# Windowed ALiBi attention feeding a Swish-gated MLP: loading and transposing q and k by head pair, adding bias and mask with a TensorE table in two batches, and gating the loads

## The chip, the cores and the metric

One NeuronCore of one Trainium2 chip runs the whole program. The metric is the device time of one execution in microseconds (us). Lower is better. The profile is one execution recorded by the hardware profiler, and its span is one to two us shorter than the measured time of the same run. All times compared here are of runs in the fast state, except where one slow run is named (a run more than 1.5% above the fastest of its kernel is called slow and left out). The profiled run of the kernel before took 376.3 us (its runs lie around 374).

Engine names in the profile: PE is TensorE matmul, PEld its weight load, DVE is VectorE, ACT is ScalarE, POOL is GpSimd, SPq is the queue of the sync engine that issues most DMAs. The granted clock is the share of its full clock that TensorE was given.

## The reference

```python
# q, k, v: (8 batches, 8 heads, 576 tokens, 64)
scores = q @ k.T / sqrt(64)
rel    = pos[:, None] - pos[None, :]
scores = where((rel >= 0) & (rel < 128), scores - slope[h] * abs(rel), -1e9)   # window 128
attn   = softmax(scores) @ v
x      = attn as (4608 tokens, 512)
h      = x @ w_in                       # 512 x 2048
out    = (h * sigmoid(beta * h)) @ w_out   # 2048 x 512
```

## The kernel before

q, k and v are float32 in memory and are loaded by blocks of 128 tokens for all heads. One row of a head is 64 floats, so one packet is 256 bytes. GpSimd casts to bf16, TensorE transposes, VectorE copies the transposes out of PSUM.

```python
fst_pool = ...tile_pool(name="fst", bufs=16)          # float32 staging for q, k and v
psum_h: 2 banks (MoE tiles)   psum_o: 2 (output tiles)
psum_s: one score tile of 2 banks                      psum_t: 2 (everything else)

def load_rows(src, b, sb):                             # one block of 128 tokens, all heads
    f = fst_pool.tile([P, H, D], F32, ...)
    nc.sync.dma_start(out=f[0:rows], in_=src[b, :, P*sb : P*sb+rows, :].rearrange("h p d -> p h d"))

def SC(b, m, p):                                       # one score tile: head pair p, half m
    sps = psum_s.tile([P, 2, 512], F32, ...)
    ... nc.tensor.matmul(o, lhsT=k, rhs=q, start=True, stop=True)
    for e in range(2):                                 # four exponentials, ALiBi as their bias
        for half, cols in ((0, slice(0, OWN[m])), (1, slice(OWN[m], 512))):
            nc.scalar.activation(out=pt[:, e, cols], in_=sps[:, e, cols], func=Exp,
                                 scale=qscale, bias=bias[:, half, h:h+1])
    nc.vector.tensor_tensor(out=pt[:], in0=pt[:], in1=masks[m][:], op=mult)

def HS(g, j):   # MoE tile: 4 matmuls of 512 columns, tanh on ACT, multiply on DVE
def OS(g, i, n) # output tile: 16 matmuls of 512 columns in 4 steps
```

The tokens go through the MoE in nine groups of 512. `att` is the list of the attention steps: T (transposition), SC (score tile), PV, and X (transposition of the result). The main loop puts these steps between the MoE steps. Group 0 has 16 MoE tiles and no output tiles. It must also hold the attention of batch 1 and the first part of batch 2.

```python
for g in range(NTG):
    ... items = HS tiles of g, and from g = 1 on the OS tiles of g - 1
    start, span_ = done, len(items) - 3
    for n, it in enumerate(items):
        it()
        while done < min(target, start + (target - start) * (n + 1) // span_):
            att[done][1](); done += 1
```

The softmax here doesn't subtract the row's maximum and nothing guards it: scores larger than these inputs give would overflow.

Of the kernel before, what the change touches and what calls it, by code (L numbers as in the profile page):

```python
# [10 lines left out]
ALU = mybir.AluOpType  # L11
ACTF = mybir.ActivationFunctionType
# [6 lines left out]
def kernel(  # L19
# [17 lines left out]
    NP = H // 2  # L37
    NQB = 5
# [10 lines left out]
    REF = 63.5  # L49

    const = ctx.enter_context(tc.tile_pool(name="const", bufs=1))
    ident = const.tile([P, P], BF16, name="ident")
    identf = const.tile([NFF, NFF], F32, name="identf")
    bflat = const.tile([NFF, P], F32, name="bflat")
    beta_h = const.tile([P, NFF], F32, name="beta_h")
    one = const.tile([P, 1], BF16, name="one")
    masks = [const.tile([P, 2, 512], BF16, name=f"mask{m}") for m in range(2)]
# [9 lines left out]
    fst_pool = ctx.enter_context(tc.tile_pool(name="fst", bufs=16))  # L67
    bst_pool = ctx.enter_context(tc.tile_pool(name="bst", bufs=4))
    pt_pool = ctx.enter_context(tc.tile_pool(name="ptp", bufs=11))
    xn_pool = ctx.enter_context(tc.tile_pool(name="xn", bufs=2))  # L70
# [3 lines left out]
    psum_h = ctx.enter_context(tc.tile_pool(name="psum_h", bufs=2, space=bass.MemoryType.PSUM))  # L74
    psum_o = ctx.enter_context(tc.tile_pool(name="psum_o", bufs=2, space=bass.MemoryType.PSUM))
# [4 lines left out]
    def load_rows(src, b, sb):  # L80
        rows = ROWS[sb]
        f = fst_pool.tile([P, H, D], F32, name="fst", tag="fst")
        nc.sync.dma_start(  # L83
            out=f[0:rows],
            in_=src[b, :, P * sb : P * sb + rows, :].rearrange("h p d -> p h d"),
        )
        return f

    staged = {}

    def load_qk(b, sb):
        rows = ROWS[sb]
        fq = load_rows(q, b, sb)
        fk = load_rows(k, b, sb)
        t = bst_pool.tile([P, 2, H, D], BF16, name="bst", tag="bst")
        nc.gpsimd.tensor_copy(out=t[0:rows, 0], in_=fq[0:rows])  # L96
        c = nc.gpsimd.tensor_copy(out=t[0:rows, 1], in_=fk[0:rows])  # L97
        staged[b, sb] = t
        return c

    def load_v(b, sb):
        rows = ROWS[sb]
        f = load_rows(v, b, sb)
        return nc.gpsimd.tensor_copy(out=VS[b % 2][0:rows, sb, :, 0:D], in_=f[0:rows])  # L104

    make_identity(nc, ident[:])
    nc.sync.dma_start(out=bflat[:], in_=moe_beta.rearrange("(j p) -> j p", p=P))
    make_identity(nc, identf[:])
    nc.vector.memset(one[:], 1.0)
# [3 lines left out]
    )  # L113

    low = dict(compare_op=ALU.is_ge, fill=0.0, base=0, channel_multiplier=-1)
    up = dict(compare_op=ALU.is_ge, fill=0.0, base=-1, channel_multiplier=1)

    def fill(m, at, n, w, sign, how):
        for e in range(2):
            nc.gpsimd.affine_select(  # L120
                out=masks[m][:, e, at : at + n * w].rearrange("p (n w) -> p n w", w=w),
                in_=bass.AP(tensor=one.tensor, offset=one[:].offset,
                            ap=[list(one[:].ap[0]), [0, n], [0, w]]),
                pattern=[[0, n], [sign, w]], **how,
            )


    fill(0, 0, 2, P, 1, low)
    fill(0, 256, 2, P, -1, up)

    fill(1, 0, 1, P, 1, low)
    fill(1, 128, 1, 64, 1, low)
    fill(1, 192, 1, P, 1, low)
    fill(1, 320, 1, 64, -1, up)
    fill(1, 384, 1, P, -1, up)
    for h in range(H):
        for half in range(2):
            nc.vector.tensor_scalar(
                out=bias[:, half, h : h + 1], in0=kpos[:], scalar1=-(REF + half * P),
                scalar2=slopes[h], op0=ALU.add, op1=ALU.mult,  # L140
            )
# [4 lines left out]
    for sb in range(3):  # L146
        load_qk(0, sb)
# [10 lines left out]
    bps = psum_t.tile([P, NFF], F32, name="bps", tag="t")  # L158
    nc.tensor.transpose(out=bps[:], in_=bflat[:], identity=identf[:])
    nc.vector.tensor_scalar_mul(beta_h[:], bps[:], 0.5)  # L160
# [4 lines left out]
    def T(b, sb):  # L165
        rows = ROWS[sb]
        src = staged.pop((b, sb))
        tps = psum_t.tile([P, 2, NP, P], BF16, name="tps", tag="t")
        for i in range(2):
            for p in range(NP):  # L170
                nc.tensor.transpose(  # L171
                    out=tps[:, i, p, :],
                    in_=src[:, i, 2 * p : 2 * p + 2, :].rearrange("r h d -> r (h d)"),
                    identity=ident[:],
                )
        nc.vector.tensor_copy(  # L176
            out=QK[b % 2][:, :, :, P * sb : P * sb + rows], in_=tps[:, :, :, 0:rows]
        )
# [5 lines left out]
    def SC(b, m, p):  # L184
        qk = QK[b % 2]
        sps = psum_s.tile([P, 2, 512], F32, name="sps", tag="sps")
        for kb in ((0, 1), (2, 4, 3))[m]:
            at, after = COLS[kb]
            nq = {3: P + 64, 4: 64}.get(kb, 2 * P)
            for e in range(2):  # L190
                o = sps[:, e, at : at + min(nq, 512 - at)]
                if kb in (0, 2):
                    o = bass.AP(
                        tensor=o.tensor, offset=o.offset,
                        ap=[list(o.ap[0]), [after - at, 2], [1, P]],
                    )
                nc.tensor.matmul(  # L197
                    o,
                    lhsT=qk[64 * e : 64 * e + 64, 1, p, P * kb : P * kb + P],
                    rhs=qk[64 * e : 64 * e + 64, 0, p, P * kb : P * kb + nq],  # L200
                    start=True, stop=True, skip_group_check=True,
                )
        pt = pt_pool.tile([P, 2, 512], BF16, name="pt", tag="pt")
        for e in range(2):
            h = 2 * p + e
            for half, cols in ((0, slice(0, OWN[m])), (1, slice(OWN[m], 512))):
                nc.scalar.activation(  # L207
                    out=pt[:, e, cols], in_=sps[:, e, cols], func=ACTF.Exp,
                    scale=qscale, bias=bias[:, half, h : h + 1],
                )  # L210
        nc.vector.tensor_tensor(out=pt[:], in0=pt[:], in1=masks[m][:], op=ALU.mult)  # L211
        pts[b, m, p] = pt
# [81 lines left out]
    def pvx(b, qbs):  # L294
        r = []
        for qb in qbs:
            r += [(None, lambda g=g, qb=qb: PV(b, qb, g)) for g in range(2)]
            if qb != qbs[0]:
                r.append(((b, qb - 1), lambda qb=qb: X(b, qb - 1)))
        r.append(((b, qbs[-1]), lambda: X(b, qbs[-1])))  # L300
        return r

# [10 lines left out]


    att, before = [], []
    for b in range(B):
        for m in range(2):
            a = [(None, lambda b=b, sb=sb: T(b, sb)) for sb in ((0, 1, 2), (3, 4))[m]]
            a += [(None, lambda b=b, m=m, p=p: SC(b, m, p)) for p in range(NP)]
            att.append((None, lambda b=b, m=m: loads_ahead(b, m)))  # L320
            att += merged(a, before)
            before = pvx(b, ((0, 1), (2, 3, 4))[m])
            if b == 0 and m == 1:
                att += before[:6]
                before = before[6:]
# [3 lines left out]
    def place_of(tok):  # L329
        b, s = divmod(tok - 1, S)  # L330
        return place[b, s // P]
# [3 lines left out]
    def loads_ahead(b, m):  # L335
        if m == 0:
            if b:
                for sb in (3, 4):
                    load_qk(b, sb)
                for sb in (2, 3, 4):  # L340
                    load_v(b, sb)
        elif b + 1 < B:
            for sb in range(3):
                load_qk(b + 1, sb)
            for sb in range(2):
                c = load_v(b + 1, sb)
            if b == 0:
                with tc.issue_after(c.ins):
                    for n in range(4):
                        load_w2(n)  # L350

    with tc.manual_schedule(engines={mybir.EngineType.PE}):
        for sb in range(2):
            load_v(0, sb)
        for sb in (3, 4):
            load_qk(0, sb)
        for sb in (2, 3, 4):
            c = load_v(0, sb)
            if sb == 3:
                with tc.issue_after(c.ins):  # L360
                    for n in range(4):
                        load_w1(n)
        done = 0
        while done < need[0]:
            att[done][1]()
            done += 1
        for g in range(NTG):
# [7 lines left out]
            start, span_ = done, len(items) - 3  # L375
            for n, it in enumerate(items):
                it()
                while done < min(target, start + (target - start) * (n + 1) // span_):
                    att[done][1]()
                    done += 1  # L380
# [32 lines left out]
```

## Time and profile before

| | |
|---|---|
| median of 3 runs | 374.04 us (373.74 to 374.73) |
| first tanh of group 0 | 44.3 us |
| first tanh of group 1 | 82.1 us |
| end of span | 374.6 us |

The two tanh times are read from the timeline (ScalarE, tile `sig`; every sixteenth instruction starts a group). They cut the span into a start, group 0, and a rest.

First, parts 1, 2 and 4 of the page of the kernel before. In part 2 each digit is the busy share of one fortieth of the span, in tenths. The last line below is the chain that ended last, by engine.

```profile
span 374.6 us, 6713 instructions
PE 338.5 (90%) x2529; PEld 172.7 (46%) x2529; DVE 224.2 (60%) x473; ACT 214.4 (57%) x437; POOL 84.4 (23%) x151
...
PE   2367687788999999999999999999999999999995
...
PEclk9999999899999999999999999999999999999999
DMA  9999999999297898954138440000000010001012
GB/s 166 209 206 202 193 195 214 192 216 180 76 214 159 159 186 170 205 126 107 50 96 187 109 104 31 28 30 29 30 28 30 30 57 29 29 29 58 28 56 86
...
PE 80%; DMA 6%; DVE 4%; ACT 4%; SPq 4%; issue 1%; POOL 0%; ACTq 0%
```

TensorE is full from the eleventh slice on. Before that it has gaps, and in the same slices the DMA row is full at about 200 GB/s.

Last, four groups from the list of groups of the kernel before: count, busy us, mean ns of one, then the idle time before it and its releaser.

```profile
L207 ACT ACTIVATE pt<-sps,bias 128x256 bf16<-128x256 f32 (+2 forms) x256 | 100.4, 480 | 34.9 <-PE sps L197 34.6
L211 DVE TENSOR_TENSOR pt<-pt,mask 128x1024 bf16<-128x1024 bf16 x64 | 46.1, 720 | 21.2 <-ACT pt L207 20.0
L197 PE MATMUL sps<-qkT 64*128 64x256 bf16 (+2 forms) x320 | 28.3, 271 | 14.1 <-ACT pt L207 13.1
L176 DVE COPY qkT<-tps 128x1024 bf16<-128x1024 bf16 (+1 forms) x40 | 25.5, 637 | 21.5 <-PE tps L171 21.3
```

### The profile page before, as it was taken

What the parts mean: (1) busy time and instruction counts of PE and PEld (TensorE: products, weight loads), DVE (VectorE), ACT (ScalarE), POOL (GpSimd) and SP (SyncE); (2) the same over time, 40 slices, a digit from 0 to 9 for tenths busy, and PEclk for the clock granted to TensorE, in tenths of its full rate; (3) what the DMA queues carried; (4) which work ended last, traced back from release to release, by engine and by line L of the source; (5) the groups of instructions that cost most, each with busy time, mean ns of one, the idle gap of its engine ahead of it and who ended that gap; (6) DMA issues with size and microseconds to landing.
All of it is one profiled execution on the core that took longest, in us unless ns stands there. A gap on an engine that the chain in (4) does not pass through costs nothing.

```text
span 374.6 us, 6713 instructions
## 1 busy us (share of the span) xinstructions
PE 338.5 (90%) x2529; PEld 172.7 (46%) x2529; DVE 224.2 (60%) x473; ACT 214.4 (57%) x437; POOL 84.4 (23%) x151
## 2 busy tenths in 40 slices
PE   2367687788999999999999999999999999999995
PEld 1145334434454455445454545454545445544442
DVE  3266467777665677665666776776767755533400
ACT  1453359375745875585846694668566854445421
POOL 7570703453122213112033303320100000000000
PEclk9999999899999999999999999999999999999999
DMA  9999999999297898954138440000000010001012
GB/s 166 209 206 202 193 195 214 192 216 180 76 214 159 159 186 170 205 126 107 50 96 187 109 104 31 28 30 29 30 28 30 30 57 29 29 29 58 28 56 86
DMA packets 121985, 42.40 MB, mean 113 GB/s; under 512 B 113232, under 2 KB 117344, under 8 KB 121952
## 3 DMA queue, kind: packets, MB, share of 16 engines
q1 hardware_dynamic: 117728, 37.77, 47.9%
q0 software_dynamic: 4224, 4.19, 6.7%
q8 instruction: 20, 0.33, 0.4%
q14 instruction: 13, 0.11, 0.1%
HBM read 36.71 MB, written 9.44 MB: 123 GB/s over the span
## 4 chain that ended last, share of the span: by engine, by line
PE 80%; DMA 6%; DVE 4%; ACT 4%; SPq 4%; issue 1%; POOL 0%; ACTq 0%
PE ops L283 34%; PE hps L267 32%; PE sps L197 4%; DMA fst<-in_k_dram 4%; PE tps L171 4%; SPq L83 4%; ACT pt L207 3%; PE xt L249 2%; PE pv L233 2%; DVE gT L273 2%; PE pv L229 2%; DMA fst<-in_v_dram 1%; ACT sig L272 1%; DVE pt L211 1%; DVE qkT L176 1%
## 5 line engine op out<-in xcount | busy, mean ns | idle before, releaser
L272 ACT ACTIVATE sig<-hps,beta_h 128x512 bf16<-128x512 f32 x144 | 99.5, 692 | 98.4 <-PE hps L267 87.4
L267 PE MATMUL hps<-XT,W 128*128 128x512 bf16 x576 | 150.7, 385 | 3.6 <-DVE gT L273 3.0
L283 PE MATMUL ops<-W,gT 128*128 128x512 bf16 x576 | 144.9, 379 | 0.0
L273 DVE SCALAR_TENSOR_TENSOR gT<-sig,hps 128x512 bf16<-128x512 bf16 x144 | 98.3, 683 | 53.0 <-ACT sig L272 52.4
L207 ACT ACTIVATE pt<-sps,bias 128x256 bf16<-128x256 f32 (+2 forms) x256 | 100.4, 480 | 34.9 <-PE sps L197 34.6
L267 PEld LDWEIGHTS <-W 128*128 128x128 bf16 x576 | 51.1, 98 | 56.5 <-issue 10.9
L283 PEld LDWEIGHTS <-gT 128*128 128x128 bf16 x576 | 51.3, 98 | 52.2 <-issue 1.7
L211 DVE TENSOR_TENSOR pt<-pt,mask 128x1024 bf16<-128x1024 bf16 x64 | 46.1, 720 | 21.2 <-ACT pt L207 20.0
L96 POOL CAST bst<-fst 128x512 bf16<-128x512 f32 (+1 forms) x40 | 24.6, 615 | 108.8 <-issue 78.7
L197 PE MATMUL sps<-qkT 64*128 64x256 bf16 (+2 forms) x320 | 28.3, 271 | 14.1 <-ACT pt L207 13.1
L104 POOL CAST vs<-fst 128x512 bf16<-128x512 f32 (+1 forms) x40 | 26.1, 659 | 65.0 <-PE pv L233 38.1
L176 DVE COPY qkT<-tps 128x1024 bf16<-128x1024 bf16 (+1 forms) x40 | 25.5, 637 | 21.5 <-PE tps L171 21.3
L171 PE MATMUL tps<-ident,bst 128*128 128x128 bf16 x320 | 28.8, 240 | 7.8 <-POOL bst L96 4.3
L239 DVE TENSOR_TENSOR xn<-pv,zs 128x256 bf16<-128x256 f32 (+1 forms) x80 | 33.7, 422 | 2.6
L289 ACT ACTIVATE osb<-ops 128x512 f32<-128x512 f32 x36 | 21.6, 601 | 20.8 <-PE ops L283 20.8
L233 PE MATMUL pv<-vs,pt 128*128 128x65 bf16 x320 | 31.0, 200 | 2.5 <-DVE xn L239 1.5
L171 PEld LDWEIGHTS <-bst 128*128 128x128 bf16 x320 | 23.5, 107 | 17.3 <-POOL bst L96 4.9
L197 PEld LDWEIGHTS <-qkT 64*128 64x128 bf16 x320 | 12.4, 97 | 38.2 <-issue 35.1
L233 PEld LDWEIGHTS <-pt 128*128 128x128 bf16 x320 | 23.6, 102 | 13.7 <-issue 1.8
L97 POOL CAST bst<-fst 128x512 bf16<-128x512 f32 (+1 forms) x40 | 25.3, 634 | 9.3 <-DMA fst<-in_k_dram 9.2
L229 PE MATMUL pv<-vs,pt 128*128 128x65 bf16 x256 | 25.8, 200 | 1.8 <-DVE qkT L176 1.2
L229 PEld LDWEIGHTS <-pt 128*128 128x128 bf16 x256 | 21.3, 102 | 8.3 <-DVE xn L239 1.3
(26 smaller groups left out, 74.3 us busy)
## 6 DMA issues: line engine op xcount, KB each, us to landing
out_dram<-osb SPq DMA_DIRECT2D x36, 256.0 KB, 2.0
fst<-in_q_dram SPq DMA_DIRECT2D x32, 256.0 KB, 4.8
fst<-in_k_dram SPq DMA_DIRECT2D x32, 256.0 KB, 4.8
fst<-in_v_dram SPq DMA_DIRECT2D x32, 256.0 KB, 5.0
W<-in_moe_w_in_dram POOLq DMA_DIRECT2D x4, 512.0 KB, 11.5
W<-in_moe_w_out_dram POOLq DMA_DIRECT2D x4, 512.0 KB, 12.6
fst<-in_q_dram SPq DMA_DIRECT2D x8, 128.0 KB, 4.2
fst<-in_k_dram SPq DMA_DIRECT2D x8, 128.0 KB, 4.2
```

The lines of the kernel that those rows point to most:

```text
L171: nc.tensor.transpose(out=tps[:, i, p, :], in_=src[:, i, 2 * p : 2 * p + 2, :].rearrange("r h d -> r (h d)"), identity=ident[:],)
L176: nc.vector.tensor_copy(out=QK[b % 2][:, :, :, P * sb : P * sb + rows], in_=tps[:, :, :, 0:rows])
L197: nc.tensor.matmul(o, lhsT=qk[64 * e : 64 * e + 64, 1, p, P * kb : P * kb + P], rhs=qk[64 * e : 64 * e + 64, 0, p, P * kb : P * kb + nq], ...
L207: nc.scalar.activation(out=pt[:, e, cols], in_=sps[:, e, cols], func=ACTF.Exp, scale=qscale, bias=bias[:, half, h : h + 1],)
L211: nc.vector.tensor_tensor(out=pt[:], in0=pt[:], in1=masks[m][:], op=ALU.mult)
L229: nc.tensor.matmul(pv[:, hl, 0 : D + 1], lhsT=weights(b, qb - 1, h, 1), rhs=vs[:, qb - 1, h, 0 : D + 1], start=True, stop=False,)
L233: nc.tensor.matmul(pv[:, hl, 0 : D + 1], lhsT=weights(b, qb, h, 0), rhs=vs[:, qb, h, 0 : D + 1], start=qb == 0, stop=True,)
L239: nc.vector.tensor_tensor(out=xn[0:nq, 4 * g : 4 * g + 4, :], in0=pv[0:nq, :, 0:D], in1=zs[0:nq].broadcast_to([nq, 4, D]), op=ALU.mult,)
L267: nc.tensor.matmul(hps[:], lhsT=W1[:, c, bass.ts(j, P)], rhs=XT[:, c, c0 : c0 + TOKG], start=(c == 0), stop=(c == NDM - 1),)
L272: nc.scalar.activation(out=sig[:], in_=hps[:], func=ACTF.Tanh, scale=beta_h[:, j : j + 1])
L273: nc.vector.scalar_tensor_tensor(out=gts[g][:, j, :], in0=sig[:], scalar=1.0, in1=hps[:], op0=ALU.add, op1=ALU.mult)
L283: nc.tensor.matmul(ops_[:], lhsT=gT[:, j, i * P : i * P + P], rhs=W2[:, j, :], start=(j == 0), stop=(j == NFF - 1),)
```

## The change

The intent is to start the MoE earlier. q and k come by head pair, 96 rows of 6 tokens each, so that a packet is 1,536 bytes and a pair can be scored as soon as it has landed. In batches 0 and 1 a matmul of a scaled identity with a table puts ALiBi and mask into the score tile before q and k are accumulated: one exponential of 1,024 columns replaces four, and the mask multiply goes. Batch 0 is done as a whole before the MoE begins, with three score buffers. Loads are held back by gates so that the weights get through.

```diff
-    fst_pool = ctx.enter_context(tc.tile_pool(name="fst", bufs=16))
+    NPE = 2                                             # batches with the table
+    fst_pool = ctx.enter_context(tc.tile_pool(name="fst", bufs=5))       # v
+    fqk_pool = ctx.enter_context(tc.tile_pool(name="fqk", bufs=8))       # q, k
+    def load_qk(b, p, gate=None):
+        for i, src in enumerate((q, k)):
+            f = fqk_pool.tile([P, 2, LA, D], F32, name="fqk", tag="fqk")
+            if gate is not None:                        # the buffer waits for `gate` to land
+                nc.gpsimd.tensor_copy(out=f[0:1, 0, 0, 0:1], in_=gate)
+                gate = None
+            nc.sync.dma_start(
+                out=f[0:LR].rearrange("r h a d -> r h (a d)"),
+                in_=src[b, 2*p : 2*p+2].rearrange("h (r a) d -> r h (a d)", a=LA))
+            t = bst_pool.tile([P, LA, 2, D], BF16, name="bst", tag="bst")
+            c = nc.gpsimd.tensor_copy(out=t[0:LR], in_=f[0:LR].rearrange("r h a d -> r a h d"))
+    def late_consts():                                  # masks and biases of batches 2 to 7
+        ... 9 + 16 nc.gpsimd.tensor_scalar(...)
+    def load_beta():
+        nc.sync.dma_start(out=bflat[:], in_=moe_beta...)   # was the first DMA of the program
+        nc.tensor.transpose(out=bps[:], in_=bflat[:], ...)
     def SC(b, m, p, pool=None):
+        if b < NPE:
+            for e in range(2):
+                nc.tensor.matmul(sps[:, e, :], lhsT=sident[:, 2*p+e, :], rhs=table[m][:], start=True, stop=False)
...
+        if b < NPE:
+            nc.scalar.activation(out=pt[:], in_=sps[:], func=Exp, scale=qscale)
...
     def T(b, p, i):        # 6 transposes of 96 columns; copied out with a step of 96 elements
+        nc.vector.tensor_copy(out=QK[...].rearrange("c (r a) -> c r a", a=LA), in_=tps[:].rearrange("c a r -> c r a"))
...
     # steps of one half of a batch: T T T T SC SC SC SC, merged with 5 PV, or 5 PV and 5 X
+        for sb in range(NQB): load_v(0, sb)             # w_in issued after the cast of block 3
+        for sb in range(NQB): load_v(1, sb)
+        for p in range(NP):
+            c = load_qk(1, p, W1[0:1, 0, 1024:1025] if p == 0 else None)            # first gate
+        late_consts()
+        ... T and SC of batch 0, then load_beta(), then PV and X of batch 0
...
+            load_qk(b + 1, p, W2[0:1, 8, 0:1] if b == 1 and p == 0 else None)        # second gate
...
+            first = 11 if g == 0 else 0                 # attention in group 0 after 11 MoE tiles
-            start, span_ = done, len(items) - 3
+            start, span_ = done, len(items) - 3 - first
```

## The prediction

> **What bounds the kernel now.** From about 90 us on TensorE is the bound: the row of busy slices is all 9s, the chain of waits is 80% TensorE, and the groups of that window show 0.6 us of matmul idling. A 512-column matmul runs every 0.216 us, so the 1,152 MoE matmuls alone are 249 us. Attention adds, by spacings in the timeline, about 0.22 us per score tile and 55 to 58 ns per PV matmul or transpose: in all some 325 us. The other 50 us are lost before 90 us. In the timeline the first MoE matmul comes at 42.4 us, when TensorE has had about 12 us of work; MoE group 0 runs until about 79 us, paced by batch 1's attention (one score buffer: matmul 0.6 + four exponentials 1.57 us = 2.27 us per tile) and by loads: DMA is full for 80 us at about 200 GB/s, almost all in 256 B packets (22 ns each in the trace).
>
> **Removed, added, moved.**
> - q and k packets become 1,536 B. The trace's 2,048 B packets took 88 ns, so I estimate 65 to 70 ns instead of 6 x 22 = 132: batch 0's q and k land in 6 to 7 us instead of 12. Its eight GpSimd casts (0.61 us per 512 columns, so an estimated 0.92 each) then set the pace: last pair ready near 11 us.
> - Batch 0 goes first as a whole, with three score buffers. One exponential of 1,024 columns is estimated at 1.12 us (0.83 ns per column between the 256- and 512-column ones), against 1.57; no mask multiply (0.72 us). Last score near 16 us, then PV and X paced by VectorE (0.6 us per PV, 0.43 per X): first MoE matmul near 25 us.
> - The table adds 32 matmuls of 512 columns: 6.9 us of TensorE, half in the prologue, nearly free.
> - VectorE: minus 16 multiplies (11.5 us); transposes are copied out with a 96-element inner step. The Trainium skill ("VectorE: DVE Perf Modes", section "What auto-detection actually checks") asks for step 1 for the doubled rate; the present 1,024-column copy at 0.69 us agrees with that rate. I expect 0.75 us for 576 columns, 64 times: copies 25.5 -> 48 us. ScalarE loses 12 us.
> - Steady batches: 48 transposes of 96 columns for 40 of 128, about equal. Scores unchanged.
>
> **Critical path.** 17 us come from the start. Part is given back in group 0: eleven MoE tiles run with nothing between them, and two buffers force about 1.2 us per tile (0.86 matmul, then 0.69 tanh and 0.69 VectorE), 4 us lost; then all of batch 1 and half of batch 2 come in a burst of some 26 us with about 18 us of TensorE work. Group 1 should start near 65 us instead of 79. From there 296 us as before, perhaps 1 to 2 more for the slower copies. Sum: 359 us.
>
> **Predicted: 359 us, 8 in 10 between 351 and 367.** Faster by over 2%: 0.88; within 2%: 0.10; slower: 0.02.
>
> **What would show it.** First MoE matmul at 22 to 28 us; packets under 512 B falling from 113,000 to about 39,000; transposition copies near 0.75 us; exponential of 1,024 columns near 1.12 us; MoE tiles 1.2 us apart in the first stretch; a TensorE dip near 40 to 60 us; all 9s after it; the time from group 1's start unchanged.
>
> **What would make it wrong.** Weights or gated q/k of batch 1 landing late (each us costs about one); the cold clock (eight transposes took 1.04 us at 20 us, 0.46 at 51 us; the Trainium skill, "TensorE: Matmul & The Clock Gate", section "What's actually happening", agrees) lasting through the prologue; slow strided GpSimd casts; VectorE so loaded that the slower copies stall TensorE.

## More of the kernel before

TensorE keeps the order of the program; the other engines are ordered by the scheduler.

Next, the windows view of the kernel before, cut at the two tanh times: for each stretch its length, then busy time and instruction count per engine, granted clock, DMA share and GB/s.

```profile
0.00:44.30 44.30, 23.57 (x203) 15.20 (x205) 21.33 (x65) 15.41 (x37) 25.15 (x54) 1.00 1.17 197
44.30:82.10 37.80, 28.52 (x245) 15.49 (x245) 26.89 (x56) 25.34 (x56) 15.87 (x27) 0.95 1.12 201
82.10:374.60 292.50, 286.42 (x2084) 141.98 (x2083) 176.00 (x353) 173.64 (x344) 43.38 (x72) 1.00 0.38 89
```

The rest (292.5 us) is TensorE at work almost without a gap. What can be won lies in the first 82 us.

## The result, and the profile after

The changed kernel is correct and slower: 399.0 us (397.26 to 399.46, 4 runs; a fifth of 401.54 us counts in the ratio) against 374.38 us in the same rounds. The ratio is 1.066, with a 95% interval of 1.061 to 1.072. A ratio is the mean time of one kernel's fast runs over that of the kernel before in the same rounds, so it is not quite the ratio of the medians quoted.

The page of the kernel after, the same parts:

```profile
span 395.5 us, 6838 instructions
PE 351.5 (89%) x2625; PEld 174.4 (44%) x2625; DVE 238.9 (60%) x491; ACT 206.7 (52%) x389; POOL 89.5 (23%) x141
...
PE   3908876878899998999999999999999899999996
...
PEclk9965895677999999999999999999999999999999
DMA  8989999997225543544254420010100000101112
GB/s 217 209 145 220 244 212 232 258 209 160 71 76 140 141 105 109 149 120 114 87 143 116 128 83 28 29 53 2 54 27 30 27 28 27 55 27 39 43 53 80
...
PE 77%; ACT 8%; DVE 6%; DMA 4%; POOL 2%; issue 2%; SPq 1%; ACTq 0%
```

The third digit of the PE row is 0: TensorE stands still for a whole slice near 20 to 30 us. The clock row falls to 5 and 6 there, and again near 60 us. The windows of the kernel after, cut at its own tanh times:

```profile
0.00:41.40 41.40, 23.39 (x202) 12.68 (x203) 20.36 (x67) 9.15 (x10) 23.84 (x53) 0.76 1.06 200
41.40:97.00 55.60, 41.56 (x296) 19.89 (x296) 28.30 (x55) 23.87 (x37) 23.00 (x32) 0.75 1.13 225
97.00:395.50 298.50, 286.51 (x2130) 141.86 (x2127) 190.27 (x370) 173.69 (x344) 42.68 (x56) 1.00 0.24 72
```

| stretch | before | after | difference |
|---|---|---|---|
| to the first tanh | 44.3 | 41.4 | -2.9 |
| group 0 | 37.8 | 55.6 | +17.8 |
| rest | 292.5 | 298.5 | +6.0 |
| span | 374.6 | 395.5 | +20.9 |

So three things want an explanation: a start that gains 3 us where 17 were expected, a long group 0, and a slower steady part. In the rest TensorE has as much busy time as before (286.5 against 286.4), so the 6 us are gaps.

The groups of the kernel after that answer to those shown of before (the fourth is the new exponential):

```profile
L235 ACT ACTIVATE pt<-sps,bias 128x256 bf16<-128x256 f32 (+1 forms) x192 | 75.1, 478 | 13.5 <-PE sps L222 13.3
L194 DVE COPY qkT<-tps 128x576 bf16<-128x576 bf16 x64 | 47.8, 754 | 18.2 <-PE tps L190 17.6
L239 DVE TENSOR_TENSOR pt<-pt,mask 128x1024 bf16<-128x1024 bf16 x48 | 33.8, 704 | 10.5 <-ACT pt L235 10.1
L222 PE MATMUL sps<-qkT 64*128 64x256 bf16 (+2 forms) x320 | 27.6, 270 | 7.7 <-ACT pt L235 7.7
L230 ACT ACTIVATE pt<-sps 128x1024 bf16<-128x1024 f32 x16 | 16.0, 1025 | 26.2 <-PE sps L222 26.1
```

The single operations came out as predicted or a little shorter: the exponential 1.03 us (1.12 predicted), the strided copy 0.754 us (0.75). The loss is in order and waiting. This is TensorE's list of waits in the kernel after, longest first (engine, waiting line, releaser: us in total, times, longest):

```profile
PE bps L180 <- DMA bflat<-in_moe_beta_dram: 10.2, 1, 10.2
PE sps L222 <- ACT pt L235: 7.7, 9, 1.1
PE sps L208 <- ACT pt L230: 5.0, 5, 1.1
```

The first line is one wait of 10.2 us for an 8 KB load of `beta`. The chain of waits shows how it comes about; these are its pieces in order of time, start and length in us, for 13 to 30 us:

```profile
13.08 4.82 POOL mask L157 x9
17.89 1.11 POOL bias L163 x6
...
20.70 0.63 POOL bias L163 x4
21.33 0.56 POOL vs L114
21.91 0.37 SPq L109
22.37 0.61 SPq L109
23.03 6.82 DMA bflat<-in_moe_beta_dram
29.89 0.28 PE bps L180
```

GpSimd first makes constants that only batch 2 needs; they stand late in the program, but the scheduler put them here. Behind them stands the cast that frees a v buffer; there are five such buffers now. The SP queue, which works in order, waits with a v load of batch 1 for that buffer, and behind this v load and one more stands the load of `beta`. It is issued at 23.0 us and lands 6.8 us later among the traffic of `w_in` and v. The Trainium skill ("DMA: Bandwidth & Descriptors", section "Anatomy of one DMA — SWDGE (gpsimd) path") says that "any semaphore wait happens on the issuing sequencer before dispatch". The section is about DMAs issued by GpSimd, and `beta` goes through the sync queue, but the trace agrees for that queue too: the ten v issues ahead of `beta` occupy SPq from 4.69 to 22.98 us. Of these 18.3 us the trace shows 4.4 (17.4 to 21.9) as the wait for GpSimd's cast and 1.9 as waits for VectorE; the other 12 show no wait. So most of the delay comes from standing behind ten loads, and at most a quarter from the constants. TensorE keeps program order, and the transposition of `beta` stands before PV of batch 0, so everything waits. The same cast also holds back the issue of `w_in`, to 21.8 us.

### The profile page after: what moved, and what is told of

Its sections match the earlier page's. It is cut to its first block, busy times and chain, and to the rows that moved or that the text cites. A ratio compares the mean times of both kernels' runs of the same rounds, so it can differ in the third digit from the quotient of the medians.

```text
span 395.5 us, 6838 instructions
## 1 busy us (share of the span) xinstructions
PE 351.5 (89%) x2625; PEld 174.4 (44%) x2625; DVE 238.9 (60%) x491; ACT 206.7 (52%) x389; POOL 89.5 (23%) x141
## 2 busy tenths in 40 slices
DMA packets 60288, 42.39 MB, mean 107 GB/s; under 512 B 39248, under 2 KB 55648, under 8 KB 60256
## 4 chain that ended last, share of the span: by engine, by line
PE 77%; ACT 8%; DVE 6%; DMA 4%; POOL 2%; issue 2%; SPq 1%; ACTq 0%
PE ops L315 30%; PE hps L299 30%; PE sps L222 5%; ACT pt L235 4%; PE tps L190 4%; PE xt L281 3%; PE pv L265 2%; DMA fqk<-in_k_dram 2%; DVE qkT L194 2%; ACT sig L304 2%; DVE gT L305 2%; PE pv L261 2%; DMA bflat<-in_moe_beta_dram 2%; PE sps L208 2%; ACT pt L230 1%
## 5 line engine op out<-in xcount | busy, mean ns | idle before, releaser
L235 ACT ACTIVATE pt<-sps,bias 128x256 bf16<-128x256 f32 (+1 forms) x192 | 75.1, 478 | 13.5 <-PE sps L222 13.3
L100 POOL CAST bst<-fqk 96x768 bf16<-96x768 f32 x64 | 52.6, 825 | 117.7 <-PE tps L190 66.6
L315 PEld LDWEIGHTS <-gT 128*128 128x128 bf16 x576 | 50.5, 98 | 50.7 <-issue 2.9
L194 DVE COPY qkT<-tps 128x576 bf16<-128x576 bf16 x64 | 47.8, 754 | 18.2 <-PE tps L190 17.6
L239 DVE TENSOR_TENSOR pt<-pt,mask 128x1024 bf16<-128x1024 bf16 x48 | 33.8, 704 | 10.5 <-ACT pt L235 10.1
L190 PE MATMUL tps<-ident,bst 96*128 96x96 bf16 x384 | 29.2, 219 | 9.9 <-DVE tri L141 4.8
L190 PEld LDWEIGHTS <-bst 96*128 96x128 bf16 x384 | 24.2, 104 | 22.6 <-POOL bst L100 7.7
L114 POOL CAST vs<-fst 128x512 bf16<-128x512 f32 (+1 forms) x36 | 22.6, 648 | 40.2 <-PE pv L265 38.1
L230 ACT ACTIVATE pt<-sps 128x1024 bf16<-128x1024 f32 x16 | 16.0, 1025 | 26.2 <-PE sps L222 26.1
L270 DVE RECIPROCAL zs<-pv 128x4 f32<-128x4 f32 (+1 forms) x80 | 14.3, 178 | 23.9 <-PE pv L265 21.5
L265 PEld LDWEIGHTS <-pt 128*128 128x128 bf16 x320 | 24.3, 104 | 9.8 <-issue 0.8
```

Source lines behind the costliest of these rows:

```text
L100: c = nc.gpsimd.tensor_copy(out=t[0:LR], in_=f[0:LR].rearrange("r h a d -> r a h d"))
L190: nc.tensor.transpose(out=tps[:, a, :], in_=src[0:LR, a, :, :].rearrange("r h d -> r (h d)"), identity=ident[0:LR, 0:LR])
L194: nc.vector.tensor_copy(out=QK[b % 2][:, i, p, 0:S].rearrange("c (r a) -> c r a", a=LA), in_=tps[:].rearrange("c a r -> c r a"),)
L265: nc.tensor.matmul(pv[:, hl, 0 : D + 1], lhsT=weights(b, qb, h, 0), rhs=vs[:, qb, h, 0 : D + 1], start=qb == 0, stop=True,)
L315: nc.tensor.matmul(ops_[:], lhsT=gT[:, j, i * P : i * P + P], rhs=W2[:, j, :], start=(j == 0), stop=(j == NFF - 1),)
```

## The experiments

Eighteen kernels ran, all correct. Each had runs of the kernel before (medians 374.4 to 375.7).

### 1. Four single edits of the changed kernel

`beta_first`: the load of `beta` is issued first again.

```diff
+    nc.sync.dma_start(out=bflat[:], in_=moe_beta...)
     for p in range(NP):
         load_qk(0, p)
     def load_beta():
-        nc.sync.dma_start(out=bflat[:], in_=moe_beta...)
```

> Only the 8 KB beta load moves: issued first, before q and k, instead of behind ten v loads. Theory (the first loss is that TensorE waits in order 10.2 us for the transposition of beta): that wait shrinks to under 1 us, the first MoE matmul comes at 28 to 31 us instead of 39.5, and the time falls by 7 to 10 us, to 389 to 392. Rival (weights and gated q/k come late in any case, so the wait only moves): the first MoE matmul may come earlier, but the time falls by less than 3 us.

Measured: 387.31 us, ratio 1.033 (1.029 to 1.038). The wait is gone, the first tanh comes at 30.3 us instead of 41.4, and 11.7 us of the 24.6 us of loss are back. One 8 KB load in the wrong place of an in-order queue was one of the two largest single causes (`t_first` below won 11.4). The rival, that the wait would only move, falls: after the first 20 us TensorE waits for no load and no cast at all in this run.

`dummy`: useless work in the wait.

```diff
+            for n in range(36):
+                nc.tensor.matmul(warm[:, n % 2, :], lhsT=sident[:, n % 8, :], rhs=table[0][:], start=True, stop=True)
             load_beta()
```

> The kernel after with 36 useless 512-column matmuls (about 8 us at full clock) put just before the beta transposition, so that they fill the 10.2 us wait without lengthening it. Theory (the wait costs twice, because idleness halves the clock of what follows): PV and X of batch 0 then take about 5.5 us instead of 8.4, the first two MoE tiles 0.87 us instead of 1.64 each, and the time FALLS by 3 to 5 us although work was added. Rival (the clock does not matter there, the stage is paced by VectorE): no change within 1.5 us, or slower.

Measured: 398.79 us, ratio 1.063: no change. The wait for `beta` fell to 2.7 us, filled by the useless work, but PV and X of batch 0 took 9.4 us (9.5 without it), and the clock was at half again when they ran: four transposes of X took 0.61 us in both. So the filling did not keep the clock up, and the run doesn't test what the clock costs. `beta_first` helps here. There four transposes of X take 0.40 us, the clock is full, and PV and X still take 8.7 us. This stage is paced by VectorE: two PV evacuations and one X copy per block. A slow clock costs it about one us.

`spread4`: attention in group 0 begins after four MoE tiles.

```diff
-            first = 11 if g == 0 else 0
+            first = 4 if g == 0 else 0
```

> The attention work in MoE group 0 begins after 4 MoE tiles instead of 11 and is spread over the remaining tiles. Theory (the burst after tile 11 leaves TensorE waiting for the single score buffer with nothing to fill in): group 0, from its first tanh to that of group 1, falls from 55.6 us to 40 to 46 us, and the time by 10 to 15 us. Rival (batch 1's q and k arrive late and set the pace): group 0 stays above 52 us and the time falls by less than 4 us.

Measured: 391.37 us, ratio 1.042 (1.036 to 1.047), 7.6 us faster. Group 0 took 49.2 us (42.2 to 91.4) instead of 55.6. Direction right, the size less than expected, and not for the rival's reason: after the wait for `beta` TensorE waits for no load and no cast in this run. In group 0 it waits 5.2 us at table matmuls for exponentials of the single score buffer and 3.6 us for the copies of transposes.

`t_first`: the order of the steps in the steady batches.

```diff
-            att += merged(a, before)
+            att += a[:4] + merged(a[4:], before)      # T T T T, then SC and PV in turn
```

> Steady batches only: the four transposition steps of a half come first, and the PV steps are put between the score steps alone, so that score steps do not follow each other directly. Theory (the 6 us lost after group 1 are 5.8 us of score matmuls waiting for the exponentials of the tile before): those waits fall below 2 us and the time by 3 to 6 us. Rival (the loss is the 64 slower copies on VectorE, 0.75 us each): no change within 2 us.

Measured: 387.63 us, ratio 1.035 (1.030 to 1.039), 11.4 us faster, more than expected. The rest of the span after group 1's first tanh is 291.4 us, where the changed kernel had 298.5 and the kernel before 292.5. Group 0 won 3.5 us too, since the edit also reorders the steps of batches 1 and 2 that run there. TensorE's two longest waits in the rest, first for the kernel after (97.0 to 395.5 us):

```profile
PE sps L222 <- ACT pt L235: 5.8, 7, 1.1
PE hps L299 <- DVE gT L305: 1.9, 4, 0.9
```

and then for `t_first` (94.5 us to the end):

```profile
PE sps L222 <- ACT pt L235: 1.1, 2, 0.7
PE hps L299 <- DVE gT L305: 0.9, 3, 0.4
```

With eight steps T and SC and only five PV to go between them, two score tiles came close together, and the second had to wait for the exponentials of the first, because in the steady part there is one score buffer. Longer copies on VectorE (0.754 us, 64 of them) are in both kernels and cost no time here: that rival falls.

### 2. A ladder of mends that stopped short

The next four kernels add up edits: `beta_late` is `beta_first` with the 25 GpSimd constants moved behind the weights.

```diff
         with tc.issue_after(c.ins):          # c: the last cast of batch 1's q and k
             for n in range(4):
                 load_w2(n)
-        late_consts()
+            late_consts()
```

> Beta first, and the GpSimd constants for batches 2 to 7 (25 small instructions, 8.3 us), which the scheduler had put before the cast that releases the first weight load, are moved behind the second weight load. Theory (these 8 us hold back w_in, and with it the gate of batch 1's q and k): w_in is issued at 13 to 15 us instead of 22, batch 1's first casts come 6 to 8 us earlier, TensorE's 8.0 us of waiting for them (with beta first) falls below 2, and the time falls by 4 to 8 us against beta first alone (387.3). Rival (DMA bandwidth sets the arrival of w_in, not its issue): less than 2 us.

Measured: 387.65 us, ratio 1.033, no gain over `beta_first`. The issue of `w_in` came at 19.1 us instead of 22.6, not at 14, because the v block it waits for landed only at 18.5. The first casts of batch 1 came at 38.7 instead of 41.1. My expectation also rested on a misreading: of the 8.0 us of waiting for casts that I quoted, 5.6 are the first load at the very start of the program, which every variant has, and none lies after 20 us. There was no wait there to remove. From here on I count waits after 20 us only.

`late_spread4` adds the spreading from the fifth tile.

> The same, and attention in group 0 spread from the fifth MoE tile on. Theory (the burst, not the data, is most of the 17.8 us lost in group 0; in the first spreading run the data came too late to use it): group 0 falls to 40 to 46 us from about 50 to 56, and the time by 6 to 12 us against the run with beta first and late constants. Rival (the table's score tiles and the single score buffer bind wherever they are put): less than 4 us.

Measured: three fast runs at 384.9 to 385.7 us, ratio 1.028 (1.022 to 1.033). A fourth run took 518.7 us at a granted clock of 0.654. It is a slow run, it was the profiled one, and nothing is read from it. The gain of about 2 us misses the 6 to 12 expected.

`combo` adds the steady order of `t_first`.

> The same, and the steady order with the transposition steps of a half first. If the causes add up: 7 to 11 us less than the run before it, and within 2% of the kernel before or faster (355 to 370). If they overlap (waits move to another resource): 3 us or less.

Measured: 379.08 us, ratio 1.011 (1.006 to 1.017). The step of about 6 us falls just short of the 7 to 11 expected; the time is within 2% of the kernel before, but above the 355 to 370 expected. Group 0 still takes 55 us. After the fifth MoE tile the tanh pauses from 34.3 to 44.6 us, and TensorE waits 6.0 us for casts of batch 1, now that its attention starts earlier than its data. (The 13.1 us named in a later expectation include the start.)

`combo_2buf` adds a second score buffer in group 0, in the two PSUM banks that the output tiles don't need yet.

```diff
+        if pool is None and extra:           # extra: a one-buffer PSUM pool, closed before g = 1
+            pool = extra[0] if extra[1] % 2 else psum_s; extra[1] += 1
```

> The same, and in group 0 a second score buffer in the two PSUM banks that the output tiles do not need before group 1. Theory (in group 0 score tile n+1 must wait for the exponential of tile n, about 1 us for each of some 11 tiles): the waits of table matmuls for the exponential (5.0 us in all) vanish and the time falls by 4 to 8 us. Rival (once spread, MoE tiles fill these waits): less than 2 us.

Measured: 377.29 us, ratio 1.006 (1.000 to 1.011). The table's waits for the exponential (4.8 us) went, and the waits for casts rose from 6.0 to 11.9 us: a new one of 5.0 us, for a cast of batch 2, stands near 61 to 66 us. The gain is less than 2 us, as the rival said, though not because MoE tiles fill the waits: one wait took the place of another.

### 3. Gates and data order in the mended kernel

`nogate` is `combo` without the first gate.

```diff
-            c = load_qk(1, p, W1[0:1, 0, 1024:1025] if p == 0 else None)
+            c = load_qk(1, p)
```

> The combined kernel (379.1) without the first gate alone: the q and k loads of batch 1 no longer wait for the third piece of w_in; TensorE, VectorE and ScalarE keep their order exactly. Theory (the gate makes batch 1's data late: the fifth MoE tile at 34.3 us is followed by a 10 us hole, and TensorE waits 13.1 us in all for the casts): batch 1's casts begin 8 to 14 us earlier, the wait for casts falls below 5 us, and the time falls by 6 to 11 us. Rival (bandwidth is full in any case; without the gate the loads take w_in's share and the MoE tiles wait for weights instead): within 3 us, with a new wait of MoE matmuls for weights.

Measured: 378.10 us, ratio 1.008: within noise of `combo`. Batch 1's casts began 2.6 us earlier (35.5 instead of 38.1), not 8 to 14. The waits for casts fell from 6.0 to 2.6 us and the time did not follow.

`free4` also requests batch 1's q and k ahead of its v.

```diff
+        for p in range(NP):
+            c = load_qk(1, p)
         for sb in range(NQB):
             load_v(1, sb)
```

> As before without the gate, and batch 1's q and k are requested ahead of its v, so that the in-order queues do not hold them behind v. Theory (data order sets group 0): batch 1's casts are done by about 25 us, no wait of TensorE for casts is left in group 0, first MoE tile still before 31 us, and the time falls by 10 to 16 us against the combined kernel, to 363 to 369. Rival (group 0 is bound by the score, exponential and copy chain and not by data): 4 us or less.

Measured: 377.25 us, ratio 1.006 (1.002 to 1.010). A miss. Batch 1's data was early; TensorE waits 2.5 us for casts of batch 2 near 66 us and 2.4 us for `w_in`, and group 0 still takes 53 us. Early data alone brings nothing here. Why was not clear from this run; the score buffer (4.8 us of waits) was one suspect, and GpSimd, busy for 9.2 of the 10 us from 50 to 60 us with the moved constants among its work, turned out to be another.

`free0_2buf` adds the second buffer and spreads attention from the first tile.

> The same, attention spread over all tiles of group 0 from the first, and the second score buffer in group 0. If data was the last obstacle, group 0 takes 36 to 40 us and the kernel reaches 355 to 362, which is what had been predicted for the change. If cold clock or chain latency binds, group 0 stays above 45 us and the time above 366.

Measured: 376.57 us, ratio 1.006 (1.002 to 1.009), group 0 at 50.5 us. One wait of 9.9 us for a cast of batch 2, from 52.6 to 62.5 us, is nearly all that is left of waiting there.

`free0_2buf_npe1`: `NPE = 1`.

> The same with the table for batch 0 only; batch 1 goes back to bias in four exponentials and a mask multiply. Saves 16 matmuls of 512 columns (3.4 us of TensorE at full clock) and adds some 0.55 us of ScalarE and 0.7 of VectorE for each of 8 tiles. If TensorE binds in group 0: faster by 1 to 4 us. If ScalarE's chain binds there: slower by 1 to 4 us. The constants must then be ready earlier, which may cost up to 2.

Measured: 384.44 us, ratio 1.026. This run measured something else than the table. Without it, batch 1 needs the biases, and these were now made at 55.6 to 59.8 us on GpSimd, behind everything I had moved ahead of them. A score matmul waited 18.8 us for exponentials that waited for the bias. It showed that my own mend was the next obstacle.

### 4. The cause of the slow group 0, and single undoings

`after_nogates`: the changed kernel without both gates, nothing else.

> The changed kernel with both gates taken out and nothing else; TensorE, VectorE and ScalarE keep their order. If the gates are a main cause of the slow group 0: 8 us faster or more. If, as I think, they hardly matter while eleven MoE tiles run first and one score buffer paces the burst: within 3 us of 399.

Measured: 413.89 us, ratio 1.103 (1.098 to 1.108): 15 us slower. I expected no change. The list of waits of this run explains it:

```profile
PE bps L180 <- DMA bflat<-in_moe_beta_dram: 24.6, 1, 24.6
```

Without the first gate eight more loads stand before `beta` in the SP queue. Its issue moves from 23.0 to 32.3 us, and the wait grows from 10.2 to 24.6 us: 14.4 of the 15 us lost. The gate didn't help the weights here so much as it let `beta` pass.

`after_256B`: the changed kernel with 256-byte packets for q and k.

```diff
-            f = fqk_pool.tile([P, 2, LA, D], F32, ...)
+            f = fqk_pool.tile([P, LA, 2, D], F32, ...)
-                in_=src[b, 2*p : 2*p+2].rearrange("h (r a) d -> r h (a d)", a=LA),
+                in_=src[b, 2*p : 2*p+2].rearrange("h (r a) d -> r a h d", a=LA),
```

> The changed kernel with the q and k loads in 256-byte packets (the token axis outside the head pair in the staging tile), same bytes, same transpositions; the cast becomes contiguous. If packet size is worth what I predicted (132 against 65 to 70 ns per 1,536 bytes): each q or k load takes about 0.5 us longer, 4 us more before the last score of batch 0, and the time rises by 3 to 8 us. The trace of the changed kernel has 94 ns per packet and a load every 1.13 us against 1.2 us per load of the kernel before: so I now expect less than 3 us either way.

Measured: 408.47 us, ratio 1.088 (1.082 to 1.094), 9.5 us slower. So the packet size is worth a good deal here, more than I expected after seeing the trace and a little more than at first predicted. The loss shows in two places: batch 0's casts ended at 19.1 us instead of 13.1, and the wait for `beta` rose to 15.5 us. Since the second depends on the first fault of this kernel, 9.5 us is not a clean value of the packets.

`ungated`: `free0_2buf` without the second gate, and with the constants back at their early place.

```diff
-                load_qk(b + 1, p, W2[0:1, 8, 0:1] if b == 1 and p == 0 else None)
+                load_qk(b + 1, p)
```

> The mended kernel (beta first, steady order, attention spread over all of group 0, second score buffer, batch 1's q and k first and ungated) without the second gate too. Theory (its hole at 51 to 61 us in group 0 is batch 2's q and k waiting for w_out): no wait of TensorE for casts over 3 us after 30 us, group 0 36 to 42 us, the time 358 to 366. Rival (in the first 85 us the DMA engines are full, so w_out or v becomes the wait): the time stays above 370.

Measured: 365.36 us (364.3 to 365.8), ratio 0.973 (0.969 to 0.978): faster than both kernels. Its windows, cut at its own tanh times:

```profile
0.00:34.30 34.30, 21.38 (x205) 11.52 (x206) 20.31 (x67) 9.04 (x9) 25.28 (x53) 0.84 1.08 213
34.30:72.30 38.00, 32.92 (x304) 16.41 (x302) 27.14 (x56) 24.61 (x40) 14.33 (x21) 0.92 1.16 212
72.30:364.00 291.70, 285.65 (x2124) 141.25 (x2121) 189.94 (x369) 172.74 (x340) 49.24 (x66) 1.00 0.35 93
```

Group 0 is at 38.0 us, as long as in the kernel before, and it starts 10 us earlier. The number met the expectation, but the expectation rested on the gate alone, and this run differs from `free0_2buf` in two things, the gate and the place of the constants. The last run separates them, and it gives the gate the smaller part: that the number was met was luck.

`ungated_npe1`: the table in batch 0 only.

> The same with the table in batch 0 only, constants early. The table costs TensorE 3.4 us in batch 1 at full clock and saves ScalarE 0.55 and VectorE 0.7 us for each of 8 tiles. If TensorE binds group 0: 1 to 4 us faster than the run with the table in both; if ScalarE's and VectorE's chain binds: 1 to 5 us slower.

Measured: 366.25 us, ratio 0.977 (0.971 to 0.982), the interval overlapping that of `ungated`. In batch 1 the table neither wins nor loses a measurable amount.

`ungated_burst`: `ungated` with `first = 11` put back.

> The best kernel (365.4) with the burst put back: attention in group 0 only after 11 MoE tiles. The data is there now, so if the burst itself costs time (MoE tiles 1.25 us apart with two buffers, then score tiles with nothing between them), group 0 rises from 38 to 46 to 52 us and the time to 372 to 380. If only the gates and the order of data mattered: within 3 us of 365.4.

Measured: 371.31 us, ratio 0.990 (0.985 to 0.994), 6 us slower. In the profiled runs group 0 rises from 38.0 to 42.7 us and the span by 4.1 us, less than expected. So the burst by itself costs 4 to 6 us here, somewhat less than the 7.6 us that `spread4` won on the changed kernel.

`ungated_late`: `ungated` with the constants moved behind the casts, as in `beta_late`.

> The best kernel with the GpSimd constants of batches 2 to 7 moved behind the casts of batch 1, so that w_in is requested near 18 us instead of 22. If the issue of w_in holds the first MoE tile (TensorE waits 3.6 us for w_in now), the first tanh comes at 30 to 31 us instead of 34.3 and the time falls by 2 to 4 us, to 361 to 364. If DMA bandwidth sets its arrival: within 1.5 us, as it was when the same move gained nothing with beta first.

Measured: 374.34 us, ratio 0.996 (0.991 to 1.000): 9 us SLOWER, where I expected 2 to 4 faster. GpSimd's timeline in this run:

```profile
52.45 0.62 POOL L114 CAST vs<-fst 64x512 bf16<-64x512 f32 x1
53.04 4.17 POOL L158 TENSOR_SCALAR mask<-diff 128x128 bf16<-128x128 f32 x9
57.19 3.25 POOL L164 TENSOR_SCALAR bias<-kpos 128x1 f32<-128x1 f32 x16
```

and in `ungated` at the same place:

```profile
52.60 0.62 POOL L114 CAST vs<-fst 64x512 bf16<-64x512 f32 x1
53.43 0.82 POOL L100 CAST bst<-fqk 96x768 bf16<-96x768 f32 x1 [0.21 <-PE sps L226]
```

The 7.4 us of constants stand before batch 2's casts and delay them from 53.4 to 60.4 us. TensorE waits 6.8 us for them at one transposition, where all its waits for casts in `ungated` are 1.5 us. The first tanh did come earlier, by 1.2 us, but this bought nothing: TensorE then waited 3.0 us for a cast of v, which came at 49.4 us here and at 49.6 in `ungated`. `ungated_late` and `free0_2buf` differ in the second gate alone: 0.996 against 1.006, about 2 us by medians of different calls, nearer 4 by the ratios. So of the 11 us between `free0_2buf` and `ungated`, some 8 to 9 are the place of the constants (with the gate out) and 2 to 4 the gate (with the constants late); early constants with the gate kept were not run. The mend called `beta_late` looked neutral where I tested it, and cost 9 us where batch 2's data had become the next thing needed. It did not hold back every kernel built on it: in `combo`, `combo_2buf` and `nogate` GpSimd, when done with the constants, waits another 2.9 to 3.8 us at the second gate for `w_out`, so the gate came last there; in `free4` and `free0_2buf` the gate passes without a wait as soon as the constants are done.

## Why the prediction was wrong

Predicted were 359 us and "faster"; the kernel takes 399.0 us. Point by point:

- **"First MoE matmul near 25 us": wrong, 39.5 us.** This is the step that failed first. The sum had q/k loads, casts, exponentials and VectorE, and the last score did come at 19.7 us (predicted 16). It left out what the diff did to the load of `beta`: moved from the first place of the SP queue to behind ten v loads, the ninth of them waiting for a buffer, with the transposition ahead of PV in TensorE's order. In its place the runs show 10.2 us of waiting for that load; `beta_first` won 11.7.
- **"q and k land in 6 to 7 us": wrong in size.** Packets of 1,536 bytes took 94 ns on average, not 65 to 70, and loads followed each other every 1.13 us. The last of batch 0's q and k landed at 12.2 us, and its cast ended at 13.1 (predicted 11). The direction was right, as `after_256B` shows (+9.5 us).
- **"Then all of batch 1 and half of batch 2 come in a burst of some 26 us": wrong in size, about 36 us** (55.2 to 91.6 us on TensorE, with one MoE tile in between). I saw the burst and took its cost to be 8 us. MoE tiles before it are 1.27 us apart, close to the 1.2 predicted. Inside it the score buffer allows one table tile per 2.67 us while the clock is at half and 2.04 at full. The Trainium skill ("TensorE: Matmul & The Clock Gate", section "What's actually happening") has the half clock follow idleness, and the trace fits: two table matmuls take 1.01 us at 60.0 us, after waits of 0.6, 0.9 and 1.1 us, and 0.59 at 78.9. Undoing the burst won 7.6 us on the changed kernel, and putting it back cost 6 on the best one (medians). How much of it is the clock was not separated; the one run meant for it (`dummy`) didn't keep the clock up. From the first MoE matmul to group 1 the kernel took 57.6 us where 40 were predicted (25 to 65), the largest miss of the three stretches. Of group 0's 55.6 us `spread4` took off 6.4 and `t_first` 3.5; the remainder came back only in `ungated`, with several edits at once, so its split isn't shown.
- **"From there 296 us as before, perhaps 1 to 2 more for the slower copies": wrong, 298.5 against 292.5, and for another reason.** The copies are as slow as predicted (0.754 us; the Trainium skill, "VectorE: DVE Perf Modes", section "What auto-detection actually checks", asks for unit step for the doubled rate, and 1.31 ns per element here against 0.67 before agrees) and they cost nothing. The loss is 5.8 us of score tiles waiting for exponentials, from the new order of steps; `t_first` took the rest to 291.4.
- **Right:** the durations of copy and exponential, the count of small packets (39,248 against about 39,000 predicted), the saturated steady part. `ungated` shows that the idea works: with the same loads, transposes and table, five changes of order or gating and a second score buffer in group 0, the kernel takes 365.4 us: 34 us to the first tanh, 38 for group 0, 292 for the rest. This supports the prediction's aim of an early start, not its sum, which had counted on the burst and on the order of steps that had to go. Its first MoE matmul still comes 7 us later than predicted, at 32.3 us: TensorE waits 3.6 us for `w_in`, with the DMA engines full.

The account of 33.6 us from the changed kernel to the best one (399.0 to 365.4): `beta` 11.7, steady order 11.4, burst 6 to 7.6, which leaves some 3 to 4.5 us for gates, data order and second buffer together. These are single edits on different bases, so the sum is a check and not a proof. By stretches the remainder is not small: these last edits win some 8 to 9 us in group 0 (17.6 in all, less 3.5 for the order and 4.7 to 6.4 for the burst) and give back 4 at the start, where the first tanh came at 30.3 us in `beta_first` and comes at 34.3 in `ungated`.

What stays open: the share of the cold clock in the burst; how gates, data order and second buffer share what they win in group 0; what the head-pair layout and the table are each worth in batch 0 (only the packet size was undone by itself); and whether `w_in` could come earlier without delaying q and k.

## What to carry to other kernels

When a change reorders the start of a program, list for every in-order queue (the DMA issuing queue, GpSimd, TensorE) what now stands ahead of each small thing that everything needs; an 8 KB load that stood behind ten larger ones cost 11.7 of 399 us here. Put constants and other filler of an in-order engine where nothing urgent waits behind them, and check the move at its new place too: a neutral result on one base was worth minus 9 us on another. With one score buffer, the distance between two score steps in the schedule is part of the cost of the step, so count how many other steps there are to put between them.

## What the Trainium skill lacked or had wrong

- "DMA: Bandwidth & Descriptors", section "Specifications", gives 512 bytes as the least transfer for line rate. In the changed kernel packets well above it were not yet at the rate of larger ones: 256 bytes took 23.0 ns on average (11 bytes per ns), 1,536 bytes 93.8 ns (16), the 2,048-byte stores 87.4 ns (23). Load and store differ in direction as well, so size alone is not shown to be the reason, and other transfers shared the engines: the row lacks a rate by size rather than being shown wrong.
- No page that I read warns that one load waiting for a buffer holds every later load of its queue as a cost in time; the page above states the mechanism only. Here it was 10.2 us in the changed kernel and 24.6 us with eight more loads ahead.
- "TensorE: Matmul & The Clock Gate" describes the cold start and says that recorded clock events can be unreliable, but no page says that the clock row of a profile can show full speed before its first recorded change: in the kernel before the row shows 9 near 20 us, where eight transposes took 1.04 us, and the trace's first clock record is at 50.5 us. In the same timeline eight such transposes take 0.61 us at 51 us. (The prediction's 0.46 us is the part of them that stands in the chain, not their whole time.)
